# Key sums taken two groups after their loads, transposes alternating with A·V, and half of the last batch's groups turned by DMA alone

## The chip, the cores and the metric

The kernel runs on 1 core of one Trainium2 chip. The time is that of the whole launch on the device, in microseconds (us), and each kernel has the median of several runs. The profile shows one more execution, whose span goes from the first to the last instruction on the core. Engines are named as in the profile: PE (TensorE matmuls), PEld (TensorE weight loads), DVE (VectorE), ACT (ScalarE), POOL (GpSimd), and SP (SyncE, whose queue issues every DMA here).

## What is computed

Attention against keys that are pooled 4x4 and projected (768 keys for 12288 queries, width 128, 4 batches), followed by a gated block: a causal convolution of 5 taps with a sigmoid makes a gate for a projected value.

```python
# attention
kv_pool = kv.reshape(B, H // 4, 4, W // 4, 4, C).mean(axis=(2, 4))
k = v = kv_pool.reshape(B, -1, C) @ w_sr          # 768 rows
s = (q @ k.transpose(0, 2, 1)) / np.sqrt(C)
s = s - s.max(-1, keepdims=True)
a = np.exp(s)
a /= a.sum(-1, keepdims=True) + 1e-09
x = a @ v                                          # (4, 12288, 128)
# gated block
gate_pre = sum(conv_w[k] * xp[:, k:k + S] for k in range(5))   # xp: 4 zeros ahead of x
out = (1 / (1 + np.exp(-gate_pre))) * (x @ w_val) @ w_out
```

## The kernel before

**Groups and steps.** The queries of a batch are cut into 24 groups of 512, so there are 96 groups. One loop over `t` runs 4 steps (`j` = 0 to 3) for each group `gi`; a step handles 128 queries against all 768 keys. The program is written in the order in which each engine shall work (`manual_schedule`): every engine takes its instructions in the order of the code, and waits where an operand or a buffer isn't ready. Everything is pipelined over groups: while the scores of group `gi` are softmaxed (`cur`), group `gi`-2 goes through A·V (`avg`), `gi`-3 through the convolution (`xg`) and `gi`-4 through the gated block (`mg`).

**One step.** `score` makes the 128x768 scores of the *next* step in 6 matmuls (q and k are split into a high and a low part), into one of three pairs of PSUM banks (tile `s`, pool `ps_s`, `bufs=3`). So the scores of step 2 take the pair that step 3 of the group before had. `row_max` (DVE, tile `nm`) finds the maxima, `expo` (ACT) the exponentials. `p_hi` (ACT) and `p_lo` (DVE, one step later) split the probabilities into two fp16 parts; `p_lo` is the last reader of `s` and sets its bank pair free.

**Turning.** A·V needs the probabilities with the keys on partitions. Steps 0 to 2 are turned by DMA: `p_hi` and `p_lo` write tile `hl`, and a `dma_start_transpose` on SP's queue writes tile `pt` (steps 0 and 1 together, step 2 alone). Step 3 is turned on PE: `expo` writes `pf` in SBUF, and `turn` transposes its six 128x128 blocks back into the bank pair, from where `p_hi` and `p_lo` write `pt`. `on_pe(j)` is `j >= 3`.

**A·V.** 18 fp16 matmuls for a group add up in one bank (`av`). `AV_CUTS` spreads them over the four steps: 7, 2, 3 and 6. After the last, `g_x` (DVE) makes `x` from `av`.

**PE's order.** In step 0: scores, 7 of A·V, and one small transpose of the row sums (`norm_turn`, tiles `z` to `m`). Step 1: scores, the value projection `g_val` (tile `m`, L388), 2 of A·V. Step 2: scores, the output projection `g_out` (L398), 3 of A·V. Step 3: scores, 6 of A·V, the six turns (L298). `g_val`, `g_out` and `norm_turn` share one PSUM bank (pool `ps_m`, `bufs=1`); `norm_store` (DVE, tile `r`) must have read the row sums before `g_val` may write.

**DVE's order.** Step 0: `row_max`, reciprocal, `p_lo` of step 3, and, when a later batch is being prepared, `pool_kv`. Step 1: `row_max`, `r`, `p_lo`, `g_h` (tile `h`, which needs `g_val`). Step 2: `row_max`, `p_lo`. Step 3: `row_max`, `p_lo`, `g_x`. ACT's order in steps 2 and 3 is `expo`, `p_hi`, the cast of a later group's queries (`g_qh`), `expo`.

**Keys of the next batch.** `setup_steps` makes a list of steps, one of which is taken at the end of each group: 16 pieces, which load part of kv (`load_kv`, tile `kvt`) and return the sum over 16 neighbours (`pool_kv`, L121, tile `pool`) as work for step 0 of the next group; then the projections and the splitting of keys and values. The first piece loads three pieces, so its sum stands one step behind its own load. The first batch's keys are made ahead of the loop. `load_moe` returns 14 small DVE instructions that convert the block's weights from 64-bit words (`convert`); 8 of them stand among the sums of the first batch, and 6 are handed out from step 6 on (`trickle`, two in a step).

Of the kernel before, what the change touches and what calls it, by code (L numbers as in the profile page):

```python
# [8 lines left out]
F16 = mybir.dt.float16  # L9
# [7 lines left out]
P = 128  # L17
GQ = 512
NT = GQ // P
NX = 3  # L20


class Group:
# [4 lines left out]
def attn_moe_kernel(ctx, tc, qT, kvT, w_sr, w_moe, outT):  # L28


    nc = tc.nc
    B, C, N = qT.shape
    RR = R * R
    NK = kvT.shape[2] // RR
    NCH = NK // P
# [3 lines left out]
    TAPS = NW - 2 * C  # L39
    HALO = TAPS - 1  # L40
    PIECES = 16
    AV_CUTS = (0, 7, 9, 12, 18)
    assert 3 * NCH == AV_CUTS[-1]
    PC = NK // PIECES
    AHEAD = 5
# [6 lines left out]
    hlp = ctx.enter_context(tc.tile_pool(name="hlp", bufs=2))  # L52
# [10 lines left out]
    def misc():  # L63
        return ps_m.tile([P, GQ], F32, name="m")
# [51 lines left out]
    def load_kv(b, st, i):  # L116
        st["kv", i] = kvp.tile([C, PC * RR], F32, name="kvt", bufs=AHEAD)
        nc.sync.dma_start(out=st["kv", i], in_=kvT[b, :, i * PC * RR:(i + 1) * PC * RR])

    def pool_kv(st, i):  # L120
        nc.vector.tensor_reduce(out=st["pool"][:, i * PC:(i + 1) * PC],  # L121
                                in_=st.pop(("kv", i)).rearrange("c (k s) -> c k s", s=RR),
                                axis=AX.X, op=ALU.add)

    def key_tiles(st):
        st["pool"] = keys.tile([C, NK], F32, name="pool", bufs=1)
        for n in ("kh", "kl"):
            st[n] = keys.tile([C, NK], F32R, name=n)
        for n in ("vh", "vl"):
            st[n] = keys.tile([P, NK], F16, name=n)  # L130
        st["vt"] = keys.tile([C, NK], F32, name="vt", bufs=1)

    def project(st, h, m):
        nc.tensor.matmul(m[:, :HALF], wsr, st["pool"][:, h * HALF:(h + 1) * HALF],
                         start=True, stop=True)
        st["m"] = m[:, :HALF]
# [55 lines left out]
        return high, low  # L192

    trickle = []

    def value_steps(st):
        return [lambda: trickle.extend(column_scale(st)), lambda: None, lambda: None,
                lambda: values(st, 0, misc()) or split_values(st, 0),
                lambda: values(st, 1, misc()) or split_values(st, 1)]

    def setup_steps(b, st):
        def piece(i):
            if i == 0:
                key_tiles(st)
            for k in range(3) if i == 0 else (i + 2,):
                if k < PIECES:
                    load_kv(b, st, k)
            return None, lambda: pool_kv(st, i)

        steps = [lambda i=i: piece(i) for i in range(PIECES)]  # L210
        steps += [lambda h=h: project(st, h, misc()) or split_keys(st, h) for h in range(2)]
        return steps + value_steps(st)

# [27 lines left out]
    def halves(a):  # L241
        return a.rearrange("p (h k) -> p h k", h=2)
# [11 lines left out]
    def row_max(g, j):  # L254
        nm = small.tile([P, 1], F32, name="nm")
        nc.vector.tensor_reduce(out=nm, in_=g.s[j], axis=AX.XY, op=ALU.max, negate=True)  # L256
        g.nm[j] = nm

    def on_pe(j):

        return j >= NX

    def expo(g, j):
        if j == 0:
            g.z = zs[g.i % len(zs)]
        if on_pe(j):
            g.pf[j] = pfp.tile([P, NK], F32, name="pf")
        nc.scalar.activation(out=halves(g.pf[j]) if on_pe(j) else g.s[j], in_=g.s[j],  # L268
                             func=AF.Exp, bias=g.nm.pop(j), accum_out=g.z[:, j:j + 1])

    def norm_eps(g):
# [18 lines left out]
        row = g.rd.rearrange("(o j) p -> o (j p)", o=1)  # L290
        nc.sync.dma_start(out=g.rb, in_=row.broadcast_to([C, GQ]))

    def turn(g, j):

        pf = g.pf.pop(j)
        for k in range(NCH):
            c = k % (NCH // 2) * P
            nc.tensor.transpose(g.s[j][:, k // (NCH // 2), c:c + P], pf[:, k * P:(k + 1) * P],  # L298
                                ident)

    def pt_tile(g):
        if g.pt is None:
# [2 lines left out]

    def part(g, j, a):

        if on_pe(j):
            return pt_tile(g)[:, j, a * NCH:(a + 1) * NCH].rearrange("p (h k) q -> p h (k q)", h=2)
        if g.hl is None:  # L310
            g.hl = hlp.tile([P, NX, 2, NK], F16, name="hl")
        return halves(g.hl[:, j, a])

    def p_hi(g, j):
# [2 lines left out]
    def p_lo(g, j):  # L317

        nc.vector.scalar_tensor_tensor(out=part(g, j, 1), in0=g.s.pop(j), scalar=2.0 ** 15,  # L319
                                       in1=part(g, j, 0), op0=ALU.mult, op1=ALU.subtract)  # L320
        if j in (1, 2):
            j0 = 0 if j == 1 else j
            nc.sync.dma_start_transpose(
                out=pt_tile(g)[:, j0:j + 1].rearrange("p j k q -> p (j k) q"),
                in_=g.hl[:, j0:j + 1].rearrange("p j a k -> p (j a k)"))
# [3 lines left out]
    def av_range(g, out, lo, hi, j0=0, j1=NT):  # L329
        for i in range(lo, hi):  # L330
            v, k, a = AV_ORDER[i]
            nc.tensor.matmul(out, g.st[v][:, k * P:(k + 1) * P], g.pt[:, j0:j1, a * NCH + k],  # L332
                             start=(i == 0), stop=(i == len(AV_ORDER) - 1))

    def av_part(g, part):
        if part == 0:
            g.av = ps_av.tile([C, GQ], F32, name="av")
        av_range(g, g.av, AV_CUTS[part], AV_CUTS[part + 1])

    def new_x(g, prev, copy):  # L340
        g.x = xp.tile([C, HALO + GQ], F32, name="x")
# [55 lines left out]
    def g_out(h, m):  # L397
        nc.tensor.matmul(m, wout, h, start=True, stop=True)  # L398
        return m
# [20 lines left out]
    for b in range(B):  # L420
        for i in range(NG):
            g = Group()
            g.i, g.b, g.t0, g.st = len(groups), b, i * GQ, states[b]
            g.s, g.nm, g.pf, g.hl, g.pt = {}, {}, {}, None, None
            groups.append(g)
    G = len(groups)
# [5 lines left out]
    st = states[0]  # L432
# [8 lines left out]
    for i in range(PIECES):  # L441
        if i + AHEAD < PIECES:
            load_kv(0, st, i + AHEAD)
        if i == 3:
            convert = load_moe()
        pool_kv(st, i)
        if i >= 8 and convert:
            convert.pop(0)()
        if i == 3 * PIECES // 4:
            low()  # L450
        if i % (PIECES // 2) == PIECES // 2 - 1:
            h = 2 * i // PIECES
            project(st, h, bank_pair()[:, 0])
            high, low = split_keys(st, h)
            high()
# [7 lines left out]
    steps = value_steps(st)  # L463
# [6 lines left out]
    for t in range(NT * G):  # L470
        gi, j = divmod(t, NT)
        cur, prev, nxt = (at(u // NT) for u in (t, t - 1, t + 1))
        last, avg, xg, mg, og = (at(gi - d) for d in (1, 2, 3, 4, 5))
        if j == 2 and gi % 2 == 0 and at(gi + 4):
            load_pair(at(gi + 4), at(gi + 5))
        if gi % NG == 1 and j == 0 and at(gi + NG - 1):
            steps += setup_steps(cur.b + 1, states[cur.b + 1])
        if t == NT + 2:
            trickle += convert

        if nxt:
            score(nxt, (j + 1) % NT)
        if mg and j == 1:
            mg.m = g_val(mg, misc())
        if mg and j == 2:
            mg.m = g_out(mg.h, misc())
        if avg:
            av_part(avg, j)

        if high and (j == 0 or t < NT):  # L490
            high()
            high = None
        row_max(cur, j)
        expo(cur, j)
        if on_pe(j):
            turn(cur, j)
            norm_eps(cur)
            if mg:
                out_tile(mg)
                g_evac(mg, mg.m)  # L500
        p_hi(cur, j)
        if mg and j == 0:
            mg.th = g_tanh(mg.gate)
        if xg and j == 1:
            tap(xg, TAPS - 1, nc.scalar)
        if last and j == 0:
            norm_reciprocal(last)
        if last and j == 1:
            norm_store(last)
        drip()  # L510
        if prev:
            p_lo(prev, (j - 1) % NT)
        if low and (j == 0 or t < NT):
            low()
            low = None
        if last and j == 0:
            norm_turn(last, misc())
        drip()
        if mg and j == 1:
            mg.h = g_h(mg.th, mg.m)  # L520
        if avg and j == 3:
            new_x(avg, xg, nc.gpsimd.tensor_copy)
            g_x(avg, avg.av)
        if xg and j == 1:
            g_conv(xg)
        if last and j == 3:
            norm_rows(last)
        if at(gi + 2) and j == 2:
            g_qh(at(gi + 2))
            g_ql(at(gi + 2))  # L530
        if og and j == 0 and og.i % 2:
            store_pair(og)
        if steps and (j == 3 or t < NT):
            high, low = steps.pop(0)() or (None, None)
# [20 lines left out]
    for i in (1, 2, 3):  # L555
        av_part(n2, i)
# [61 lines left out]
```

## Time and profile before

| | |
|---|---|
| median of 3 runs | 1132.18 us (1131.02 to 1132.25) |
| the profiled execution: its time | 1133.22 us |
| its span | 1131.4 us |
| PE busy | 1063.6 us, 94% of the span |
| DVE, ACT, POOL busy | 919.0, 910.4, 864.4 us (81%, 80%, 76%) |
| mean granted TensorE clock | 0.983 |
| DMA: share of the 16 engines | 85.4%, mean 190 GB/s |

A busy PE is not PE at its peak: matmuls overlap in the records. What a piece of work costs on PE is read from the chain of waits, which strings PE's pieces together end to start. An engine's idle time ahead of an instruction stands behind it in brackets in the timeline, with the engine that ended it; where that engine had long been done, it was another.

### The profile page before, as it was taken

How to read it: one execution, taken by the hardware profiler on the slowest of the kernel's cores; microseconds unless marked ns; L12 is line 12 of the kernel's file. 1: busy time of each engine (PE TensorE's matmuls, PEld its weight loads, DVE VectorE, ACT ScalarE, POOL GpSimd, SP SyncE). 2: the span in 40 equal slices, each digit the busy share in tenths (PEclk: the TensorE clock that was granted, in tenths of full speed). 3: DMA queues.
4: the chain of work that ended last, by engine and by line, in shares of the span. 5: the costliest groups of instructions: out<-in, count | busy, mean ns of one | idle time of the engine just before them, and what ended most of it. 6: DMA issues, size and time to landing. Idle time of an engine off the chain costs nothing.

```text
span 1131.4 us, 16595 instructions
## 1 busy us (share of the span) xinstructions
PE 1063.6 (94%) x5174; PEld 715.6 (63%) x5174; DVE 919.0 (81%) x1290; ACT 910.4 (80%) x1659; POOL 864.4 (76%) x948
## 2 busy tenths in 40 slices
PE   2879999999979999999997999999999999999996
PEld 1656666666756666666764666666666666666663
DVE  6868888888858888888885888888888888888884
ACT  1868888888858888888885888888888888888881
POOL 1168788878858888888885888887888888888872
PEclk9989999999989999999998999999999999999998
DMA  7779999887879999888876999898788888888872
GB/s 271 145 178 200 211 210 232 192 178 191 187 169 198 202 224 214 206 177 191 187 165 170 209 217 226 200 221 183 171 171 197 187 170 202 186 170 199 175 148 93
DMA packets 487095, 215.53 MB, mean 190 GB/s; under 512 B 453088, under 2 KB 453856, under 8 KB 487008
## 3 DMA queue, kind: packets, MB, share of 16 engines
q1 hardware_dynamic: 487008, 214.48, 85.4%
q8 instruction: 41, 0.67, 0.2%
q14 instruction: 46, 0.38, 0.1%
HBM read 75.83 MB, written 25.36 MB: 89 GB/s over the span
## 4 chain that ended last, share of the span: by engine, by line
PE 49%; DVE 25%; ACT 11%; issue 6%; POOL 5%; DMA 3%; SPq 1%; DVEq 0%; ACTq 0%
PE s L250 17%; PE av L332 16%; PE m L388 8%; DVE nm L256 8%; POOL ql L236 5%; ACT s L268 5%; DVE pool L121 4%; DVE pt L319 4%; ACT hl L315 4%; DVE x L349 4%; PE m L398 3%; PE s L298 3%; DMA kvt<-in_kv 3%; ACT qh L232 2%; DVE h L393 2%
## 5 line engine op out<-in xcount | busy, mean ns | idle before, releaser
L368 POOL TENSOR_TENSOR sum<-sum,tap 128x512 f32<-128x512 f32 x282 | 359.6, 1275 | 39.7 <-ACT tap L357 17.8
L332 PE MATMUL av<-pt,vh 128*128 128x512 f16 x1140 | 389.1, 383 | 0.0
L256 DVE TENSOR_REDUCE nm<-s 128x1 f32<-128x768 f32 x384 | 364.4, 949 | 3.7 <-PE s L250 3.7
L268 ACT ACTIVATE s<-s,nm 128x768 f32<-128x768 f32 x288 | 251.9, 875 | 125.5 <-DVE nm L256 124.3
L359 POOL TENSOR_SCALAR tap<-x,wm 128x512 f32<-128x512 f32 x376 | 253.4, 693 | 82.4 <-DVE x L349 80.9
L319 DVE SCALAR_TENSOR_TENSOR hl<-s,hl 128x768 f16<-128x768 f32 x288 | 273.1, 948 | 21.0 <-ACT hl L315 20.3
L250 PE MATMUL s<-kh,qh 128*128 128x384 f32 x768 | 253.3, 411 | 10.8 <-DVE hl L319 8.1
L315 ACT ACTIVATE hl<-s 128x768 f16<-128x768 f32 x288 | 233.3, 810 | 9.1
L332 PEld LDWEIGHTS <-vh 128*128 128x128 f16 x1164 | 114.0, 98 | 175.5 <-issue 85.8
L332 PE MATMUL av<-pt,vl 128*128 128x512 f16 x570 | 217.5, 382 | 0.0
L236 POOL TENSOR_TENSOR ql<-q,qh 128x512 fp32r<-128x512 f32 x96 | 121.8, 1269 | 122.6 <-ACT qh L232 122.6
L250 PE MATMUL s<-kh,ql 128*128 128x384 f32 x768 | 199.1, 341 | 0.0
L250 PE MATMUL s<-kl,qh 128*128 128x384 f32 x768 | 198.9, 340 | 0.0
L250 PEld LDWEIGHTS s<-kh,qh 128*128 128x128 f32 x768 | 132.4, 193 | 51.8 <-DVE hl L319 8.4
L349 DVE SCALAR_TENSOR_TENSOR x<-av,down,rb 128x512 f32<-128x512 f32 x95 | 71.4, 751 | 89.6 <-POOL ql L236 71.5
L250 PEld LDWEIGHTS s<-kl,qh 128*128 128x128 f32 x768 | 141.3, 190 | 0.5 <-DVE kl L147 0.5
L250 PEld LDWEIGHTS s<-kh,ql 128*128 128x128 f32 x768 | 140.9, 190 | 0.0
L388 PE MATMUL m<-x,wm 128*128 128x512 f32 x188 | 103.0, 630 | 25.0 <-DVE r L285 24.9
L368 POOL TENSOR_TENSOR sum<-tap,tap 128x512 f32<-128x512 f32 x94 | 120.4, 1281 | 0.0
L393 DVE SCALAR_TENSOR_TENSOR h<-th,m 128x512 f32<-128x512 f32 x94 | 64.7, 689 | 59.2 <-PE m L388 57.7
L315 ACT ACTIVATE pt<-s 128x768 f16<-128x768 f32 x96 | 77.8, 810 | 37.8 <-PE s L298 37.8
L332 PEld LDWEIGHTS <-vl 128*128 128x128 f16 x582 | 57.6, 99 | 77.9 <-issue 55.2
(68 smaller groups left out, 1068.9 us busy)
## 6 DMA issues: line engine op xcount, KB each, us to landing
kvt<-in_kv SPq DMA_DIRECT2D x64, 384.0 KB
rb<-rd SPq DMA_DIRECT2D x96, 256.0 KB
q<-in_q SPq DMA_DIRECT2D x47, 512.0 KB
out<-o SPq DMA_DIRECT2D x46, 512.0 KB
pt<-hl SPq DMA_TRANSPOSE x192
rd<-r SPq DMA_DIRECT2D x96, 2.0 KB
out<-o SPq DMA_DIRECT2D x3, 256.0 KB
q<-in_q SPq DMA_DIRECT2D x2, 256.0 KB
```

The lines of the kernel that those rows point to most:

```text
L236: nc.gpsimd.tensor_tensor(out=g.ql, in0=g.q, in1=g.qh.bitcast(F32), op=ALU.subtract)
L250: nc.tensor.matmul(s[:, h, :HALF], a[:, sl], k[:, h * HALF:(h + 1) * HALF], start=(i == 0), stop=(i == 2))
L256: nc.vector.tensor_reduce(out=nm, in_=g.s[j], axis=AX.XY, op=ALU.max, negate=True)
L268: nc.scalar.activation(out=halves(g.pf[j]) if on_pe(j) else g.s[j], in_=g.s[j], func=AF.Exp, bias=g.nm.pop(j), accum_out=g.z[:, j:j + 1])
L315: nc.scalar.activation(out=part(g, j, 0), in_=g.s[j], func=AF.Copy, scale=2.0 ** 15)
L319: nc.vector.scalar_tensor_tensor(out=part(g, j, 1), in0=g.s.pop(j), scalar=2.0 ** 15, in1=part(g, j, 0), op0=ALU.mult, op1=ALU.subtract)
L332: nc.tensor.matmul(out, g.st[v][:, k * P:(k + 1) * P], g.pt[:, j0:j1, a * NCH + k], start=(i == 0), stop=(i == len(AV_ORDER) - 1))
L349: nc.vector.scalar_tensor_tensor(out=g.x[:, HALO + c0:HALO + c1], in0=av, scalar=g.st["down"], in1=g.rb[:, c0:c1], op0=ALU.mult, op1=ALU.mult)
L359: eng.tensor_scalar(out=g.tap[k], in0=src, scalar1=w, scalar2=1.0, op0=ALU.mult, op1=ALU.mult)
L368: nc.gpsimd.tensor_tensor(out=s, in0=acc, in1=g.tap[k], op=ALU.add)
L388: nc.tensor.matmul(m, wval, g.x[:, HALO + c0:HALO + c1], start=True, stop=True)
L393: nc.vector.scalar_tensor_tensor(out=h, in0=th, scalar=1.0, in1=m, op0=ALU.add, op1=ALU.mult)
```

## The change

It has five parts.

1. `pool_kv` no longer stands in step 0 right after its load. A piece's sum is put into a list when the next piece is loaded, and one sum is taken from the list in each step 2. A sum so comes two groups behind its load, and the list of steps is one longer (17 pieces).
2. `AV_CUTS` goes from 7, 2, 3, 6 to 6, 2, 2, 8 matmuls in steps 0 to 3.
3. The six turns of step 3 no longer follow the A·V matmuls: each of them is issued behind one of the last six.
4. In the last batch, every second group (0, 2, 4 ...) is turned by DMA in all four steps; its steps 2 and 3 go together. Tile `hl` holds four steps now.
5. The 14 converting instructions all stand in the loop, from step 4 on.

```diff
-    AV_CUTS = (0, 7, 9, 12, 18)
+    AV_CUTS = (0, 6, 8, 10, 18)
...
         def piece(i):
             if i == 0:
                 key_tiles(st)
+            else:
+                pooling.append(lambda: pool_kv(st, i - 1))
             for k in range(3) if i == 0 else (i + 2,):
                 if k < PIECES:
                     load_kv(b, st, k)
-            return None, lambda: pool_kv(st, i)
-        steps = [lambda i=i: piece(i) for i in range(PIECES)]
+        steps = [lambda i=i: piece(i) for i in range(PIECES + 1)]
...
-        return j >= NX
+        return j >= g.by_dma
...
-        if j in (1, 2):
-            j0 = 0 if j == 1 else j
+        if (j % 2 or j == g.by_dma - 1) and not on_pe(g, j):
+            j0 = j // 2 * 2
...
+        lo, hi = AV_CUTS[part], AV_CUTS[part + 1]
+        for i in range(lo, hi):
+            av_range(g, g.av, i, i + 1)
+            if hi - i <= len(between):
+                between.pop(0)()
...
+            g.by_dma = 4 if b == B - 1 and i % 2 == 0 else 3
...
-        if i >= 8 and convert:
-            convert.pop(0)()
...
-        if t == NT + 2:
+        if t == 3:
             trickle += convert
...
+        row_max(cur, j)
+        expo(cur, j)
+        turns = turn_steps(cur, j) if on_pe(cur, j) else []
         if avg:
-            av_part(avg, j)
+            av_part(avg, j, turns)
...
+        if pooling and j == 2:
+            pooling.pop(0)()
```

What this does to the engines' queues is seen at three places. First PE in step 3 of a group in the middle of the program. `av<-pt,vh` and `av<-pt,vl` are A·V matmuls with the high and low part of the values, each behind its weight load, `s<-ident,pf` a turn, `s<-kh,qh` the first matmul of the next scores. Before, the last three of step 3's six A·V matmuls, the turns, and the next scores:

```order
L332 LDWEIGHTS vh
L332 MATMUL av<-pt,vh 128x512
L332 LDWEIGHTS vl
L332 MATMUL av<-pt,vl 128x512
L332 LDWEIGHTS vh
L332 MATMUL av<-pt,vh 128x512
L298 MATMUL s<-ident,pf 128x128 [waits Activation_49]
L298 MATMUL s<-ident,pf 128x128 x5
L250 MATMUL s<-kh,qh 128x384 [waits DVE_49,PE_49]
```

After, the first four of step 3's eight, with the first turns between:

```order
L251 MATMUL s<-kh,ql 128x384
L336 LDWEIGHTS vl
L336 MATMUL av<-pt,vl 128x512
L336 LDWEIGHTS vh
L336 MATMUL av<-pt,vh 128x512
L336 LDWEIGHTS vh
L336 MATMUL av<-pt,vh 128x512
L300 MATMUL s<-ident,pf 128x128 [waits Activation_49]
L336 LDWEIGHTS vl
L336 MATMUL av<-pt,vl 128x512
L300 MATMUL s<-ident,pf 128x128
```

The first turn, which waits for ACT's exponentials, stood behind six A·V matmuls of its step and now stands behind three; five A·V matmuls stand behind it.

Second DVE, from `p_lo` of step 3 (`pt<-s,pt`) to the next `g_x` (`x`), while a later batch's keys are summed. `nm` are the row maxima, `hl<-s,hl` the other `p_lo`. Before:

```order
L319 SCALAR_TENSOR_TENSOR pt<-s,pt 128x768
L121 TENSOR_REDUCE pool<-kvt 128x48
L256 TENSOR_REDUCE nm<-s 128x1
L285 COPY r<-m 4x128
L319 SCALAR_TENSOR_TENSOR hl<-s,hl 128x768
L393 SCALAR_TENSOR_TENSOR h<-th,m 128x512
L256 TENSOR_REDUCE nm<-s 128x1
L319 SCALAR_TENSOR_TENSOR hl<-s,hl 128x768
L256 TENSOR_REDUCE nm<-s 128x1
L319 SCALAR_TENSOR_TENSOR hl<-s,hl 128x768
L349 SCALAR_TENSOR_TENSOR x<-av,down,rb 128x512
```

After:

```order
L323 SCALAR_TENSOR_TENSOR pt<-s,pt 128x768
L257 TENSOR_REDUCE nm<-s 128x1
L286 COPY r<-m 4x128
L323 SCALAR_TENSOR_TENSOR hl<-s,hl 128x768
L404 SCALAR_TENSOR_TENSOR h<-th,m 128x512
L257 TENSOR_REDUCE nm<-s 128x1
L323 SCALAR_TENSOR_TENSOR hl<-s,hl 128x768
L120 TENSOR_REDUCE pool<-kvt 128x48
L257 TENSOR_REDUCE nm<-s 128x1
L323 SCALAR_TENSOR_TENSOR hl<-s,hl 128x768
L360 SCALAR_TENSOR_TENSOR x<-av,down,rb 128x512
```

The sum of keys moved from ahead of `r` to ahead of the row maxima of step 3.

Third PE in step 3 of a group of the last batch that has no turns, after the change: the end of the eight A·V matmuls.

```order
L336 LDWEIGHTS vl
L336 MATMUL av<-pt,vl 128x512
L336 LDWEIGHTS vh
L336 MATMUL av<-pt,vh 128x512
L251 MATMUL s<-kh,qh 128x384 [waits DVE_49,PE_49]
```

Before the change this place read like the first listing above.

More of the change, by code (lines that the diff above doesn't have):

```diff
@@ L19 @@
 NT = GQ // P
-NX = 3
 class Group:
@@ L194, in attn_moe_kernel @@
     trickle = []
+    pooling = []
     def value_steps(st):
@@ L257, in row_max, with on_pe @@
         g.nm[j] = nm
-    def on_pe(j):
-        return j >= NX
+    def on_pe(g, j):
+        return j >= g.by_dma
     def expo(g, j):
@@ L265, in expo @@
             g.z = zs[g.i % len(zs)]
-        if on_pe(j):
+        if on_pe(g, j):
             g.pf[j] = pfp.tile([P, NK], F32, name="pf")
-        nc.scalar.activation(out=halves(g.pf[j]) if on_pe(j) else g.s[j], in_=g.s[j],
+        nc.scalar.activation(out=halves(g.pf[j]) if on_pe(g, j) else g.s[j], in_=g.s[j],
                              func=AF.Exp, bias=g.nm.pop(j), accum_out=g.z[:, j:j + 1])
@@ L291, in norm_rows, with turn_steps, block @@
         nc.sync.dma_start(out=g.rb, in_=row.broadcast_to([C, GQ]))
-    def turn(g, j):
+    def turn_steps(g, j):
         pf = g.pf.pop(j)
-        for k in range(NCH):
+        def block(k):
             c = k % (NCH // 2) * P
@@ L299, in turn @@
                                 ident)
+        return [lambda k=k: block(k) for k in range(NCH)]
     def pt_tile(g):
@@ L306, in part @@
     def part(g, j, a):
-        if on_pe(j):
+        if on_pe(g, j):
             return pt_tile(g)[:, j, a * NCH:(a + 1) * NCH].rearrange("p (h k) q -> p h (k q)", h=2)
         if g.hl is None:
-            g.hl = hlp.tile([P, NX, 2, NK], F16, name="hl")
+            g.hl = hlp.tile([P, NT, 2, NK], F16, name="hl")
         return halves(g.hl[:, j, a])
@@ L333, in av_range, with av_part @@
                              start=(i == 0), stop=(i == len(AV_ORDER) - 1))
-    def av_part(g, part):
+    def av_part(g, part, between=()):
         if part == 0:
             g.av = ps_av.tile([C, GQ], F32, name="av")
-        av_range(g, g.av, AV_CUTS[part], AV_CUTS[part + 1])
+        lo, hi = AV_CUTS[part], AV_CUTS[part + 1]
[3 more added lines that the diff above has]
+                between.pop(0)()
+        for matmul in between:
+            matmul()
     def new_x(g, prev, copy):
@@ L486, in attn_moe_kernel @@
             mg.m = g_out(mg.h, misc())
+        row_max(cur, j)
+        expo(cur, j)
+        turns = turn_steps(cur, j) if on_pe(cur, j) else []
         if avg:
-            av_part(avg, j)
+            av_part(avg, j, turns)
+        else:
+            for matmul in turns:
+                matmul()
         if high and (j == 0 or t < NT):
@@ L492, in attn_moe_kernel @@
             high = None
[L493 to L496, printed above, removed]
+        if j == NT - 1:
             norm_eps(cur)
```

## The prediction

> **What bounds the kernel now.** I read the page first (PE busy 94% of the span, the others 76 to 81%), then the chain of waits to see whether PE works without a break, and then the timeline of one group for the queues behind PE. From the chain of waits, one whole group of the last batch, from one set of turns to the next (start, length, piece):
>
> ```profile
> 1070.46 1.05 PE s L250 x6
> 1071.51 1.53 PE av L332 x7
> 1073.04 0.11 PE m L278
> 1073.14 1.07 PE s L250 x6
> 1074.21 0.86 PE m L388 x2
> 1075.07 0.43 PE av L332 x2
> 1075.51 1.05 PE s L250 x6
> 1076.55 0.86 PE m L398 x2
> 1077.41 0.65 PE av L332 x3
> 1078.06 1.05 PE s L250 x6
> 1079.11 1.31 PE av L332 x6
> 1080.42 0.66 PE s L298 x6
> 1081.08 1.05 PE s L250 x6
> ```
>
> PE's pieces follow each other with no hole: 10.62 us for a group (1070.46 to 1081.08). Scores are 1.05, an A·V matmul 0.218 (1.53 / 7), a turn 0.11 (0.66 / 6). PE is the bound here, but what matters for this change is how near the other engines run behind it. The timeline of another group of that batch, the rows that lead from the value projection to the turns:
>
> ```profile
> 904.04 1.02 PE L388 MATMUL m<-x,wm 128*128 128x512 f32 x2
> 905.17 0.69 DVE L393 SCALAR_TENSOR_TENSOR h<-th,m 128x512 f32<-128x512 f32 x1 [0.51 <-PE m L388]
> 905.77 0.95 DVE L256 TENSOR_REDUCE nm<-s 128x1 f32<-128x768 f32 x1
> 906.82 0.88 ACT L268 ACTIVATE s<-s,nm 128x768 f32<-128x768 f32 x1 [0.58 <-DVE nm L256]
> 907.50 0.95 DVE L256 TENSOR_REDUCE nm<-s 128x1 f32<-128x768 f32 x1
> 907.84 0.81 ACT L315 ACTIVATE hl<-s 128x768 f16<-128x768 f32 x1
> 908.55 0.61 ACT L232 CAST qh<-q 128x512 fp32r<-128x512 f32 x1
> 909.06 0.90 ACT L268 ACTIVATE pf<-s,nm 128x768 f32<-128x768 f32 x1
> 910.03 0.38 PE L332 MATMUL av<-pt,vh 128*128 128x512 f16 x1
> 910.10 0.72 PEld L298 LDWEIGHTS s<-ident,pf 128*128 128x128 f32 x6 [0.19 <-ACT pf L268]
> 910.24 0.82 PE L298 MATMUL s<-ident,pf 128*128 128x128 f32 x6
> 910.51 0.75 DVE L349 SCALAR_TENSOR_TENSOR x<-av,down,rb 128x512 f32<-128x512 f32 x1 [0.87 <-POOL ql L236]
> ```
>
> Read it as a chain: DVE waits 0.51 for the value projection before `h`; behind `h`, in DVE's order, come the maxima of step 2; ACT waits 0.58 for these, then does the exponentials of step 2, `p_hi`, the cast of q, and the exponentials of step 3 without a pause; the turns' weight load waits 0.19 for those. From the projection's start to the first turn it takes 910.24 - 904.04 = 6.20 us. PE's own work over the same stretch, from the chain of waits, is 0.86 + 0.43 + 1.05 + 0.86 + 0.65 + 1.05 + 1.31 = 6.21. So the data arrive just when PE has done its six A·V matmuls: there is no slack at all, though no wait of PE shows it.
>
> **Parts 2 and 3, the turns among A·V.** After the change PE reaches the first turn after 2 A·V matmuls in step 2 (one less) and 3 in step 3 (three less): 6.21 - 4 x 0.218 = 5.34 us. The exponentials still take 6.20, since nothing in their chain gets shorter. PE waits 0.86 at the first turn, and everything behind it in its queue (five A·V matmuls, then the scores) waits too. The wait isn't won back: the next projection stands behind the turns on PE, and the next exponentials behind the projection. It is a loop, 6.20 from projection to first turn, and then PE's path back: six turns 0.66, five A·V 1.09, scores 1.05, six A·V 1.31, the small transpose 0.11, scores 1.07 = 5.29. Together 11.49, against 10.62.
>
> In that path back stands a second wait. For it, the rows of DVE one group earlier:
>
> ```profile
> 899.90 0.75 DVE L349 SCALAR_TENSOR_TENSOR x<-av,down,rb 128x512 f32<-128x512 f32 x1 [0.87 <-POOL ql L236]
> 901.51 0.93 DVE L319 SCALAR_TENSOR_TENSOR pt<-s,pt 128x768 f16<-128x768 f32 x1
> ```
>
> `x` starts 0.48 after the last A·V matmul (910.03 to 910.51), and `p_lo` of step 3 starts 1.61 after `x` and takes 0.93. The last A·V matmul now starts 5 x 0.11 + 4 x 0.218 = 1.42 behind the first turn, so `p_lo` ends at 1.42 + 0.48 + 1.61 + 0.93 = 4.44 and its bank pair is free some 0.07 later, at 4.51. PE wants that pair for the scores of step 2 at 0.66 + 1.09 + 1.05 + 1.31 + 0.11 = 4.22: a wait of 0.29. A group with turns then takes 11.49 + 0.29 = 11.78, say 11.77 unrounded.
>
> Does alternating itself change PE's work? No row shows a turn between two A·V matmuls. The nearest is the small transpose behind seven A·V matmuls, 0.11 in the chain of waits, like a turn in a run; I take 0.11. From below, a turn streams 128 columns where an A·V matmul streams 512 in 0.218, so 0.054; from above I double it to 0.22 for the switching.
>
> The Trainium skill, "TensorE: Matmul & The Clock Gate", Step-by-step: what each phase is for, says that PE pulls weight loads ahead of matmuls in flight; by that a turn's weights would load behind A·V and the turn would cost its columns alone, which the first rival prices. The small transpose, which stands behind A·V and still takes 0.11, does not bear this out.
>
> **Part 1, the sums of keys.** Around the start of a batch's preparation the timeline shows:
>
> ```profile
> 317.56 0.75 DVE L349 SCALAR_TENSOR_TENSOR x<-av,down,rb 128x512 f32<-128x512 f32 x1 [0.87 <-POOL ql L236]
> 320.79 1.38 SPq L118 DMA_DIRECT2D kvt<-in_kv  x3
> 326.78 0.95 DVE L121 TENSOR_REDUCE pool<-kvt 128x48 f32<-128x768 f32 x1 [6.67 <-DMA kvt<-in_kv]
> 328.84 2.08 PE L388 MATMUL m<-x,wm 128*128 128x512 f32 x2 [6.97 <-DVE r L285]
> 337.66 0.75 DVE L349 SCALAR_TENSOR_TENSOR x<-av,down,rb 128x512 f32<-128x512 f32 x1 [2.11 <-issue]
> ```
>
> The list of waits has all of this kind (us in total, times, longest):
>
> ```profile
> DVE pool L121 <- DMA kvt<-in_kv: 25.2, 8, 7.0
> ```
>
> The sum waits 6.67 for a load issued 6 us before; DVE's whole queue waits behind it, then PE behind `r`, and PE starts again slowly (2.08 for a projection that takes 1.02 above). From `x` to `x` this group takes 20.10. Ordinary groups while keys are summed:
>
> ```profile
> 206.58 0.75 DVE L349 SCALAR_TENSOR_TENSOR x<-av,down,rb 128x512 f32<-128x512 f32 x1 [0.86 <-POOL ql L236]
> 209.04 0.94 DVE L121 TENSOR_REDUCE pool<-kvt 128x48 f32<-128x768 f32 x1
> 210.76 0.27 DVE L285 COPY r<-m 4x128 f32<-4x128 f32 x1
> 211.08 1.13 PE L388 MATMUL m<-x,wm 128*128 128x512 f32 x2 [0.20 <-DVE r L285]
> 217.68 0.75 DVE L349 SCALAR_TENSOR_TENSOR x<-av,down,rb 128x512 f32<-128x512 f32 x1 [0.89 <-POOL ql L236]
> ```
>
> take 11.10, since the sum delays `r` and PE waits for it. The stall is worth 20.10 - 11.10 = 9.0, three times (batches 2 to 4 are prepared in the loop): 27. Bounds: the bare waits, three of about 6.7 or 20, and 27; the first stall falls into the filling of the pipeline, where less is lost, so I take 26. Two groups are 22 us, over three times the 6 us that the load took, so no new wait takes its place on SP or DVE.
>
> The sum's new place costs something. In step 2 it stands ahead of the maxima of step 3, which started at 907.50. A sum takes DVE 0.86 to the next instruction; so they start at 908.36, end 0.95 later, and the exponentials, which started at 909.06, start at about 909.34: 0.28 more on the loop. A group with a sum takes 12.05. The wait for `r` goes: with the sum gone from ahead of it, `r` comes at the time that PE gets through the wait for the bank pair.
>
> **Part 4, the last batch.** A group without turns saves 0.66 and has no wait at a first turn. From the projection's start PE comes to the end of A·V at 0.86 + 0.43 + 1.05 + 0.86 + 0.44 + 1.05 + 8 x 0.218 = 6.43; `x` starts at 6.43 - 0.22 + 0.48 = 6.69, and `p_lo` of step 3 sets the bank pair free at 6.69 + 1.61 + 0.93 + 0.07 = 9.30. PE is there at 6.43 + 1.05 + 1.31 + 0.11 = 8.90, waits 0.40, and with 1.07 of scores the group takes 10.37. Alternating with 11.77, the mean is 11.07. The added transposes are a sixth more than now. In the table of windows the last batch's DMA share is the figure before the GB/s:
>
> ```profile
> 899.90:1070.00 170.10, 170.10 (x852) 116.78 (x850) 139.74 (x193) 149.33 (x273) 146.88 (x161) 1.00 0.86 184
> ```
>
> 0.86 while PE never stops; even if all of that were transposes, a sixth more would stand at 1.00 of the old group time, below 1.00 of the longer one. They are issued a whole group before A·V reads them, so I price them at 0.
>
> **Part 5, the conversions.** By group of lines:
>
> ```profile
> L90 DVE TENSOR_SCALAR rest<-raw 128x261 int32<-128x261 int32 x3 | 0.9, 287 | 0.0
> ```
>
> Eight such instructions leave the way to the first scores, 8 x 0.2 beyond what overlaps: at most 1.6 saved if DVE bounds there, 0 if the loads do; the same eight come back in the first groups. Between -1.6 and +1.6 I take 0.
>
> **The sum.** 48 groups with a sum (3 x 16): 12.05 - 11.10 = 0.95, +45.6. 24 groups of the last batch: 11.07 - 10.62 = 0.45, +10.8. About 20 others (92 groups have the loop, counted from the first with a value projection): before between 10.62 and 11.10, and as they too do extra work on DVE I take 11.10; 0.67 each, +13.4. Stalls at the three starts: -26. Together +44. The profiled execution took 1133.2 (span 1131.4), 1.0 above the median, so the median goes from 1132.2 to 1176.
>
> **The rivals.** *Hidden turns:* alternated turns cost 0.054. The last A·V matmul starts at 1.14, the bank pair comes at 4.23, and the loop is 6.20 + 4.23 + 1.07 = 11.50, 0.27 less in each of the 80 groups with turns (48 + 20 + 12): 1154. For it speaks only that streaming is no longer than that; against it the small transpose.
>
> *Costly switches:* five turns at 0.22 add 0.55 x 80 = 44: 1220. No row has a switching cost: A·V behind the output projection starts on time in the chain of waits.
>
> *No wait at the first turn* (faster): the exponentials are not tied to the projection, and move forward with PE. Then a group with turns is 10.62 + 0.29 = 10.91, with the wait for `r` gone: 48 x -0.19, 20 x -0.19, the last batch (10.91 + 10.37) / 2 = 10.64, +0.5, and -26 give -38: 1094. It is faster as long as the wait at the first turn is under 38 / 80 = 0.48 on the mean. For it: in the list of waits PE itself now hardly waits there. Against it: the unbroken rows from `h` to the turns.
>
> *The stalls stay:* if the sums still wait for their loads, +26: 1202. It would take loads of 20 us.
>
> **How the numbers follow.** Forecast 0.64, hidden turns 0.13, costly switches 0.09, no wait at the first turn 0.09, stalls that stay 0.02, about no change 0.03 (part of the wait, with free turns). 1176 is the first. The range reaches to hidden turns below and to half of the switching cost and the staying stalls above: 1150 to 1204. A change under 0.2% cannot be told from none here. Faster 0.10, same 0.02, slower 0.88.
>
> **What would show it.** The first turn's weight load should wait for ACT's `pf` about 1 us in 80 groups; `x` to `x` should be near 12.05 with sums, 11.8 without, and 10.4 and 11.8 by turns in the last batch; scores should wait 0.3 for `p_lo`; no sum should wait for its load in the loop. If PE shows no wait ahead of the turns, I am wrong on the loop; if the groups are right by number but 0.3 off, on the turns' cost.

## The result, and the profile after

The changed kernel takes 1202.29 us (median of 4 runs, 1201.38 to 1203.26) against 1132.22 for the kernel before: a ratio of 1.062, with a 95% interval from 1.0601 to 1.0638. The direction, the mechanism and the range (1150 to 1204) held; the point, 1176, was 26 us too low.

The head of its page:

```profile
span 1201.5 us, 16475 instructions
PE 1085.4 (90%) x5102; PEld 701.1 (58%) x5102; DVE 915.6 (76%) x1290; ACT 910.4 (76%) x1659; POOL 865.9 (72%) x948
```

Every engine has a smaller share of a longer span, which points to waits between them. Rows of the changed kernel's list of waits (us in total, times, longest):

```profile
PEld s L300 <- ACT pf L269: 95.4, 84, 1.6
PEld s L251 <- DVE pt L323: 30.8, 67, 0.6
PEld m L279 <- DVE kl L146: 9.1, 6, 1.5
PEld m L279 <- DVE vl L188: 7.9, 8, 1.3
DVE pool L120 <- DMA kvt<-in_kv: 5.6, 6, 2.8
```

The first row is the first turn (L300), which now waits for `pf` in every group with turns; its weight load did so for about 1.1 us each (95.4 / 84). The second row is the wait for the bank pair that `p_lo` of step 3 frees, 0.46 each. The next two rows were not in the prediction: the small transpose (L279) waits for the split of keys and values. The last was 25.2 before; what is left of it is the first batch, so the three stalls are gone.

The chain of waits in the last batch shows the loop whole, from one value projection (L399) to the next:

```profile
1097.39 0.87 PE m L399 x2
...
1098.35 0.69 DVE h L404
1099.04 0.88 DVE nm L257
...
1100.00 1.00 ACT s L269 x2
...
1101.03 0.81 ACT hl L319
1101.84 0.51 ACT qh L233
1102.35 0.90 ACT pf L269 x2
...
1103.29 0.33 PE s L300
1103.62 0.22 PE av L336
1103.84 0.11 PE s L300
...
1105.26 0.73 DVE x L360
...
1106.94 0.86 DVE pt L323
1107.84 1.31 PE s L251 x6
1109.15 0.86 PE m L399 x2
```

Down to `pf` it is the predicted chain: projection, `h`, maxima, exponentials, `p_hi`, the cast of q, exponentials. Then PE's turns alternate with A·V, and behind the last of them the chain leaves PE again: `x`, `p_lo` of step 3 (`pt`), and the scores that wait for its bank pair. From 1097.39 to 1109.15 is 11.76, where the prediction said 11.77.

How the 70 us (spans 1131.4 and 1201.5) come together, from the start of `x` in one group to its start in the next, in both traces:

| part of the program | predicted | measured |
|---|---|---|
| a group with a sum | 12.05 (was 11.10) | 12.05 |
| a group that only has turns | 11.77 (was 10.62) | 11.77 |
| last batch, with turns / all by DMA | 11.77 / 10.37 | 11.82 / 10.52 |
| groups with sums, the starts' included | +45.6 (48 groups) | about +48.6 (50 groups) |
| projecting keys and values, and their neighbours | +13.4 (20 groups at 0.67) | about +30 (21 groups at 1.44) |
| last batch | +10.8 | +13.1 |
| stalls at three starts | -26 | about -25 |
| up to the first `x` | 0 | +3.2 |

### The profile page after: what moved, and what is told of

Same layout as the page of the kernel before. It is cut to its first block, busy times and chain, and to the rows that moved or that the text cites. A ratio compares the mean times of both kernels' runs of the same rounds, so it can differ in the third digit from the quotient of the medians.

```text
span 1201.5 us, 16475 instructions
## 1 busy us (share of the span) xinstructions
PE 1085.4 (90%) x5102; PEld 701.1 (58%) x5102; DVE 915.6 (76%) x1290; ACT 910.4 (76%) x1659; POOL 865.9 (72%) x948
## 4 chain that ended last, share of the span: by engine, by line
POOL 32%; DVE 17%; PE 17%; issue 17%; ACT 15%; DMA 1%; POOLq 0%; DVEq 0%; ACTq 0%
POOL sum L379 15%; POOL tap L370 11%; DVE x L360 6%; PE s L251 5%; PE av L336 5%; POOL ql L237 5%; DVE nm L257 5%; ACT s L269 5%; ACT hl L319 4%; ACT pf L269 3%; PE s L300 3%; PE m L399 2%; DVE h L404 2%; DMA kvt<-in_kv 1%; ACT qh L233 1%
## 5 line engine op out<-in xcount | busy, mean ns | idle before, releaser
L336 PE MATMUL av<-pt,vh 128*128 128x512 f16 x1140 | 380.7, 381 | 0.1
L269 ACT ACTIVATE s<-s,nm 128x768 f32<-128x768 f32 x300 | 261.9, 873 | 114.1 <-DVE nm L257 101.3
L323 DVE SCALAR_TENSOR_TENSOR hl<-s,hl 128x768 f16<-128x768 f32 x300 | 284.4, 948 | 10.1 <-ACT hl L319 10.1
L251 PE MATMUL s<-kh,qh 128*128 128x384 f32 x768 | 246.0, 401 | 19.9 <-DVE hl L323 6.8
L319 ACT ACTIVATE hl<-s 128x768 f16<-128x768 f32 x300 | 243.4, 811 | 8.7
L300 PE MATMUL s<-ident,pf 128*128 128x128 f32 x504 | 141.2, 284 | 54.2 <-ACT pf L269 54.2
L251 PEld LDWEIGHTS s<-kh,qh 128*128 128x128 f32 x768 | 125.4, 191 | 102.1 <-DVE pt L323 30.8
L319 ACT ACTIVATE pt<-s 128x768 f16<-128x768 f32 x84 | 68.1, 811 | 111.5 <-PE s L300 111.5
L300 PEld LDWEIGHTS s<-ident,pf 128*128 128x128 f32 x504 | 71.0, 142 | 100.1 <-ACT pf L269 95.4
L336 PEld LDWEIGHTS <-vl 128*128 128x128 f16 x582 | 61.7, 106 | 67.6 <-issue 47.0
```

The costliest lines, as they stand in the source:

```text
L251: nc.tensor.matmul(s[:, h, :HALF], a[:, sl], k[:, h * HALF:(h + 1) * HALF], start=(i == 0), stop=(i == 2))
L269: nc.scalar.activation(out=halves(g.pf[j]) if on_pe(g, j) else g.s[j], in_=g.s[j], func=AF.Exp, bias=g.nm.pop(j), accum_out=g.z[:, j:j + 1])
L319: nc.scalar.activation(out=part(g, j, 0), in_=g.s[j], func=AF.Copy, scale=2.0 ** 15)
```

## The experiments

All were run beside the kernel before, which had medians from 1132.1 to 1133.6 in these comparisons. "A group" is `x` to `x`. The theory is the loop of the prediction; the main rivals are that turns cost something by themselves when they stand among A·V, that the sums' new place is what hurts, and that the wait at the first turn is the whole story.

**Which part does it.** First the sums alone: the kernel before with part 1.

```diff
+            else:
+                pooling.append(lambda: pool_kv(st, i - 1))
...
+        if pooling and j == 2:
+            pooling.pop(0)()
```

> The kernel before with part 1 alone: a sum of keys two groups behind its load, in step 2. Loop theory (the path from the value projection over h, the maxima, the exponentials to the first turn takes 6.20 us, and PE's way back sets the rest): the three stalls go (-26), and a group with a sum takes 6.20 + 0.28 + 4.42 = 10.90 instead of 11.10 (-0.2 x 48 = -10): 1096 us. Rival, the sum fits into idle time of DVE in step 2 and costs nothing: groups at 10.62, 1083 us. Rival, a sum in step 2 delays the turns by its full 0.86: 11.48, 1124 us.

Measured 1093.91, ratio 0.9664 (0.9649 to 0.9678). Part 1 alone is a gain of 38 us: the stalls go, and a group with a sum takes 10.83 in place of 11.10.

Then the changed kernel with its turns in a row behind the eight A·V matmuls, and the same with the old cuts, which leaves out parts 2 and 3 altogether (only the split `high` stays where the change put it):

```diff
-            if hi - i <= len(between):
-                between.pop(0)()
```

> The changed kernel with the six turns in a row behind all eight A.V matmuls of step 3 (cuts 6, 2, 2, 8 kept). Loop theory: PE reaches the first turn at 5.34 + 5 x 0.218 = 6.43 us after the projection, later than the 6.20 of the data, so the wait at the first turn goes, and x comes early enough that the bank pair isn't waited for: 10.62 without, about 10.68 with a sum, 10.5 on the mean in the last batch: about 1090 us. Rival, the cuts or the sums' place make the groups long: near 1200 us. Rival, alternating by itself costs PE time: both waits stay and only PE's own pieces get shorter, 1160 us.

```diff
-            if hi - i <= len(between):
-                between.pop(0)()
-    AV_CUTS = (0, 6, 8, 10, 18)
+    AV_CUTS = (0, 7, 9, 12, 18)
```

> The changed kernel without parts 2 and 3: cuts 7, 2, 3, 6 and the turns in a row. Loop theory: PE reaches the first turn at 6.21, the data are there at 6.20 without and 6.48 with a sum, so a group with a sum takes 10.90, 0.2 more than with cuts 6, 2, 2, 8 in a row: about 1097 us, 7 to 10 us slower than that kernel. Rival, the cuts make no difference when the turns stand in a row: the two are the same within 2 us.

Measured 1097.51 (ratio 0.9697, 0.9683 to 0.9712) and 1095.14 (0.9673, 0.9659 to 0.9687). Taking the alternation away gives back 105 of 1202 us, and with it the whole loss. But the second expectation had the order wrong: I thought the cuts 6, 2, 2, 8 would be 7 to 10 better, and they are 2.4 worse. They gain 0.15 in a group with a sum (10.68 against 10.83) and lose more elsewhere: 10.67 against 10.61 without one, 12.05 against 11.75 in a group that projects keys, 10.65 against 10.46 as the mean of twenty groups of the last batch. With one A·V matmul fewer in steps 0 and 2, PE comes to the next scores before `p_lo` has freed their banks; the list of waits of the run with 6, 2, 2, 8 in a row has it as

```profile
PEld s L251 <- DVE hl L323: 30.4, 91, 1.2
```

With the old cuts in a row this wait is 3.0 us in 5.

Parts 2 and 3 by themselves, on the kernel before (with the split `high` behind the exponentials, as the change's code has it):

> The kernel before with parts 2 and 3 alone (cuts 6, 2, 2, 8 and alternating turns); sums stay in step 0 right behind their loads, turns by DMA and conversions as before. Loop theory: p_lo of step 3 now ends 4.4 behind the first turn, the sum stands behind it and ahead of r, so the next projection can start 6.5 behind the first turn and the group with a sum takes 6.20 + 6.5 = 12.7; groups of the last batch 11.77. Against before: 45 x 1.6 = 72, 24 x 1.15 = 28, and 30 for the groups that project keys and values (three times the 10 that the changed kernel lost there): 1132 + 130 = 1262. Rival (the sums' new place is what lengthens their groups to 12.05, alternating alone leaves them at 11.77): 45 x 0.67 = 30 in place of 72, 1220.

Measured 1261.63, ratio 1.1141 (1.1122 to 1.116): 128 us slower. A group with a sum takes 12.63, one of the last batch 11.77. Where the sum stands decides what the alternation costs: in step 0 it holds `r`, and with it the projection from which the loop starts. Its weight load waits for `r` in the 15 ordinary groups with a sum from 70 to 300 us for 13.7 us in all, where it waited 7.7 in the kernel before; in the whole run, the starts included:

```profile
PEld m L397 <- DVE r L285: 54.5, 48, 6.3
```

Parts 4 and 5 by themselves, on the kernel before:

> The kernel before with part 4 alone (every second group of the last batch turned by DMA in all four steps). By the prediction's way of working, a group without turns saves 0.66 of PE and loses some to the wait for the bank pair. In the runs with turns in a row, two groups of the last batch take 10.60 + 10.28 against 2 x 10.61: 0.34 less for a pair, 12 pairs, 4.1 less: 1128. Rival (the added transposes get in the way of the others on the DMA queue, whose share in that batch was 0.86 already): no gain or a loss, 1132 or more.

> The kernel before with part 5 alone (all 14 conversions in the loop from step 4 on). The prediction took 0 between -1.6 and +1.6. The traces since show the first x 1.4 later where the conversions stand in the loop: 1133.6. Rival 1 (loads set the first scores, the groups that take the conversions have room): 1132. Rival 2 (the way to the first scores gets shorter by the eight conversions): 1130.6.

Part 4: 1127.92, ratio 0.9956 (0.9943 to 0.9968), a gain of 5.2; 3.6 of it lie in 21 groups of the last batch. Part 5: 1135.11, ratio 1.0021 (1.0011 to 1.003), a loss of 2.0; the first `x` comes 1.43 later. Rows of before, from its timeline and its windows (the granted clock stands ahead of the DMA share):

```profile
23.50 1.65 PE L134 MATMUL s<-pool,wsr 128*128 128x384 f32 x2 [7.98 <-DVE pool L121]
...
45.00:55.00 10.00, 9.28 (x53) 6.64 (x52) 9.90 (x17) 8.39 (x17) 1.26 (x1) 1.00 1.10 203
```

With part 5 alone:

```profile
22.14 1.65 PE L134 MATMUL s<-pool,wsr 128*128 128x384 f32 x2 [6.96 <-DVE pool L121]
53.78 0.88 ACT L268 ACTIVATE s<-s,nm 128x768 f32<-128x768 f32 x1 [1.39 <-DVE nm L256]
...
45.00:55.00 10.00, 9.21 (x43) 6.93 (x43) 8.62 (x17) 6.49 (x14) 0.73 (x1) 0.83 0.97 184
```

The projection of the first keys does start 1.36 earlier, as supposed. But the conversions now stand in DVE's queue while the pipeline fills: ACT waits 1.39 for maxima behind them, and PE has a granted clock of 0.83 in ten us where it had 1.00. By the first `x` more is lost than was gained; which of the two weighs more was not separated.

**What the loop is made of.** The theory says that it runs through ACT's cast of q, and that only in groups without a sum; with a sum the maxima of step 3 come last. So the cast (with `g_ql` on POOL, which reads it) is moved behind the exponentials of step 3, in the changed kernel:

```diff
-        if at(gi + 2) and j == 2:
-            g_qh(at(gi + 2))
-            g_ql(at(gi + 2))
...
         expo(cur, j)
+        if at(gi + 2) and j == 3:
+            g_qh(at(gi + 2))
+            g_ql(at(gi + 2))
         turns = turn_steps(cur, j) if on_pe(cur, j) else []
```

> The changed kernel, with the cast of the queries (g_qh on ACT and g_ql on POOL) moved from step 2 to step 3, behind the exponentials that the first turn waits for. Loop theory: without a sum the exponentials of step 3 then wait for the maxima alone, 0.5 less, so such groups take 11.27 in place of 11.77; with a sum the maxima of step 3 end at the same time as before, so those groups stay at 12.05. 12 alternating groups of the last batch and about 20 others x 0.5 = 16 less: 1186. Rival 1, the first turn isn't tied to ACT's order: no change, 1202. Rival 2, ACT's order alone sets the loop, with or without a sum: 80 x 0.5 less, 1162.

Measured 1186.00, ratio 1.0471 (1.045 to 1.0492): the loop's number. Groups with a sum stay at 12.05, those with turns only fall to 11.25. Its timeline:

```profile
1064.73 0.94 DVE L257 TENSOR_REDUCE nm<-s 128x1 f32<-128x768 f32 x1
1065.77 0.90 ACT L269 ACTIVATE pf<-s,nm 128x768 f32<-128x768 f32 x1
1066.65 0.62 ACT L233 CAST qh<-q 128x512 fp32r<-128x512 f32 x1
1066.81 0.33 PE L300 MATMUL s<-ident,pf 128*128 128x128 f32 x1
```

The exponentials follow the maxima at once, the cast comes after, and PE waits less at the first turn. Together with the 95.4 us of waits above, this rules out the rival in which the exponentials move with PE.

Then the other half of the claim, that a sum lengthens the loop since it stands ahead of those maxima. In the changed kernel the exponentials of such a group do wait for them:

```profile
212.02 0.90 ACT L269 ACTIVATE pf<-s,nm 128x768 f32<-128x768 f32 x1 [0.19 <-DVE nm L257]
```

The changed kernel with its sums in step 3, between `p_lo` and `x`:

```diff
-        if pooling and j == 2:
+        if pooling and j == 3:
```

> The changed kernel (alternating turns, cuts 6, 2, 2, 8) with the sum of keys in step 3, between p_lo and x, in place of step 2. Loop theory: the sum lay on the loop only since it stood ahead of the maxima of step 3 (0.28); DVE waits 2.17 for the last A·V ahead of x, so in the new place it is hidden and groups with a sum fall from 12.05 to 11.77: 48 x 0.28 = 13.4 less, 1189. Rival 1 (groups with a sum are long for POOL's taps or for another reason than the sum's place on DVE): 1202. Rival 2 (the sum holds x, and with it the bank pair of step 3): 1210.

Measured 1189.47, ratio 1.0495 (1.0474 to 1.0515). Groups with sums fall to 11.77, so it was the sum's place on DVE and not POOL's work that made them longer, and DVE still idles behind the sum:

```profile
209.67 0.94 DVE L120 TENSOR_REDUCE pool<-kvt 128x48 f32<-128x768 f32 x1
212.17 0.75 DVE L360 SCALAR_TENSOR_TENSOR x<-av,down,rb 128x512 f32<-128x512 f32 x1 [1.55 <-issue]
```

Is the wait at the first turn the whole story? If so, more A·V matmuls ahead of it should pay:

```diff
-    AV_CUTS = (0, 6, 8, 10, 18)
+    AV_CUTS = (0, 4, 5, 6, 18)
```

> The changed kernel with 4, 1, 1 and 12 A·V matmuls in steps 0 to 3 (in place of 6, 2, 2, 8); turns still alternate, now with the last six of twelve. Loop theory: PE reaches the first turn two A·V matmuls later, so its wait there falls from about 0.86 to 0.42; but the last turn and the last A·V come as before behind the first turn, and only 4 A·V matmuls are left in step 0 to hide p_lo, so the wait for the bank pair at the scores of step 2 grows from 0.29 to 0.73. The sum of the two waits stays, so group times stay at 11.77 and 12.05 and the time at 1202, within 6 us. Rival (only the wait at the first turn matters, the bank pair comes early enough): 80 groups x 0.44 less, 1167.

Measured 1217.96, ratio 1.0754 (1.0736 to 1.0771): slower than the change by 16, where I had said the same. The rival is refuted by far; the theory was right in part. Groups with a sum stay at 12.05 to the hundredth, since what PE no longer waits for at the turns it waits for at the scores:

```profile
PEld s L251 <- DVE hl L323: 116.5, 180, 1.2
PEld s L251 <- DVE pt L323: 43.2, 67, 0.7
PEld s L300 <- ACT pf L269: 22.1, 52, 1.2
```

Other groups took 0.16 more, and those turned by DMA alone 11.38 in place of 10.52, most of the 16 us. I had priced the bank pair of step 3 (`pt`) and not those of steps 0 to 2 (`hl`), which wait more than it does: with one A·V matmul each in steps 1 and 2, nothing covers `p_lo` there.

**The term that was too small.** In the changed kernel, a group that projects keys took 13.30:

```profile
276.53 0.75 DVE L360 SCALAR_TENSOR_TENSOR x<-av,down,rb 128x512 f32<-128x512 f32 x1 [2.41 <-PE s L300]
278.17 0.88 ACT L269 ACTIVATE s<-s,nm 128x768 f32<-128x768 f32 x1 [0.80 <-DVE nm L257]
279.06 0.48 ACT L142 ACTIVATE kh<-m 128x384 fp32r<-128x384 f32 x1
279.96 0.56 DVE L146 SCALAR_TENSOR_TENSOR kl<-m,kh 128x384 fp32r<-128x384 f32 x1 [0.89 <-ACT vt L143]
280.57 0.33 PE L279 MATMUL m<-ident,z 128*128 128x128 f32 x1 [1.03 <-DVE kl L146]
289.83 0.75 DVE L360 SCALAR_TENSOR_TENSOR x<-av,down,rb 128x512 f32<-128x512 f32 x1 [2.42 <-PE s L300]
```

The projected keys lie in the one small bank; `kh`, `vt` and `kl` read them, and the small transpose wants the same bank. In the changed code ACT does its exponentials first, which wait 0.80 for the maxima, and the split after them; before, the split went first. Put back:

```diff
+        if high and (j == 0 or t < NT):
+            high()
+            high = None
         row_max(cur, j)
         expo(cur, j)
...
-        if high and (j == 0 or t < NT):
-            high()
-            high = None
```

> The changed kernel with the block that splits projected keys and values (high, on ACT) put back ahead of the row maxima and the exponentials, as in the kernel before; the rest is as changed. Theory from the trace: the groups that project keys and values take 12.7 to 13.3 because that split now comes behind an exponential on ACT, so kl and vl are late and the small transpose, which shares their bank, waits. With the split ahead these groups should take 11.8 to 12.4: 12 groups x about 0.9 less, 1191 (1186 to 1195). Rival (what these groups lose comes from alternating itself): no change, 1202.

Measured 1191.55, ratio 1.052 (1.0501 to 1.0539). The group that took 13.30 takes 12.30, and PE hardly waits for `kl` (its weight load 3.3 us in the whole run, where it was 9.1):

```profile
275.71 0.75 DVE L360 SCALAR_TENSOR_TENSOR x<-av,down,rb 128x512 f32<-128x512 f32 x1 [2.41 <-PE s L300]
278.17 0.55 DVE L146 SCALAR_TENSOR_TENSOR kl<-m,kh 128x384 fp32r<-128x384 f32 x1
278.77 0.33 PE L279 MATMUL m<-ident,z 128*128 128x128 f32 x1
288.01 0.75 DVE L360 SCALAR_TENSOR_TENSOR x<-av,down,rb 128x512 f32<-128x512 f32 x1 [2.41 <-PE s L300]
```

**A better kernel.** The changed kernel without parts 2 and 3, and the sums in step 3:

```diff
-        if pooling and j == 2:
+        if pooling and j == 3:
```

> As the kernel with cuts 7, 2, 3, 6 and turns in a row, but the sum of keys stands in step 3, between p_lo and x, where DVE waits 0.87 for the end of A.V. Loop theory: the sum takes 0.86 there, the maxima of step 3 are no longer behind it, and a group with a sum takes 10.62 instead of 10.90: 48 x 0.28 = 13 us less, about 1084 us. Rival, DVE has no room left in any step (the sum only moves the wait to x): the same as with the sum in step 2, about 1097 us.

Measured 1083.89, ratio 0.9577 (0.9561 to 0.9593). Last, this with the split ahead of the maxima and the conversions among the first sums again:

> A version put together from the runs so far: the changed kernel with the turns in a row behind A·V and the cuts 7, 2, 3, 6 of before, the sum of keys in step 3 between p_lo and x, the conversions of the weights again among the first sums, and the split of projected keys and values (high) ahead of the maxima; the turns of the last batch by DMA as changed. Against the run with the sums in step 3 (1083.9): the first x should come 1.5 earlier, as it does where the conversions stand among the first sums; the groups that project keys should take 11.3 in place of 11.75, six groups x 0.45 = 2.7 less. 1079.7. Rival (neither place matters once PE doesn't wait at the turns): 1084.

Measured 1079.22, ratio 0.9526 (0.9512 to 0.9539): 54 us faster than the kernel before and 123 faster than the change. One of its groups with a sum:

```profile
202.64 0.94 DVE L120 TENSOR_REDUCE pool<-kvt 128x48 f32<-128x768 f32 x1
203.10 0.38 PE L336 MATMUL av<-pt,vh 128*128 128x512 f16 x1
203.32 0.82 PE L300 MATMUL s<-ident,pf 128*128 128x128 f32 x6
203.59 0.75 DVE L358 SCALAR_TENSOR_TENSOR x<-av,down,rb 128x512 f32<-128x512 f32 x1
214.20 0.75 DVE L358 SCALAR_TENSOR_TENSOR x<-av,down,rb 128x512 f32<-128x512 f32 x1
```

PE goes from A·V into the turns without a wait, the sum fills the time in which DVE waited for `x`, and the group takes 10.61: with a sum in it, what the kernel before took without one.

## Why the prediction was right, and where it was off

**The loop at the first turn: shown.** Both group times came out as predicted to the hundredth, the chain of waits goes through the named instructions, and the two runs that take one link out (the cast, the sum) moved just the groups that they should: 11.77 to 11.25 without a sum, 12.05 to 11.77 with one. What held was the step "there is no slack at all, though no wait of PE shows it". That the sums agree to the hundredth is in part luck: in the group of the chain above, the timeline has the first turn 6.06 behind the projection (1097.23 to 1103.29; the prediction said 6.20), the scores that wait for the bank pair 4.55 behind that (4.51), and the next projection 1.15 behind them (1.07). The prediction had read its 6.20 to the first turn, which stood behind PE's own A·V matmuls; the weight load, which waits for the data, started 6.06 behind the projection in the kernel before too (904.04 to 910.10). The differences cancel.

**What alternating costs by itself: nothing, nor does it save.** In the changed kernel's timeline:

```profile
213.23 0.38 PE L336 MATMUL av<-pt,vl 128*128 128x512 f16 x1
213.23 0.14 PEld L300 LDWEIGHTS s<-ident,pf 128*128 128x128 f32 x1
213.45 0.27 PE L300 MATMUL s<-ident,pf 128*128 128x128 f32 x1
213.56 0.38 PE L336 MATMUL av<-pt,vh 128*128 128x512 f16 x1
```

From a turn to the A·V matmul behind it is 0.11, as in a run. That disposes of both rivals on the turns' cost. The turn's weight load starts with the A·V matmul ahead of it (213.23), as the Trainium skill, "TensorE: Matmul & The Clock Gate", Step-by-step: what each phase is for, has it; yet the turn does not get cheaper.

**The stalls: right.** About 25 us came back (26 predicted). The rival in which they stay had 1202 for its time, which is what was measured; but no sum waits for its load inside the loop, so the number agrees by chance.

**The projecting groups: the term that was mis-sized.** About 20 groups at 0.67 each were to make +13.4; 21 groups made about 30. The prediction took 11.10 as their time before and 11.77 as that after. It had not asked where their extra work lies: before, those that project took 11.3, some 0.7 more than a group without, and in the loop the projection, issued behind the turns, stands on PE's path back, and most of the 0.7 comes on top of the 11.77 (12.30 with the split ahead). And the diff moved the split of keys and values on ACT, which the prediction did not price at all: 10.7 us (1202.29 - 1191.55), as the run with the split ahead shows. That 1202 still lies within the range is luck in part: its upper end was made of half a switching cost and of stalls that stay, and neither came.

**The first `x`: priced at 0, measured +3.2.** The bounds of -1.6 to +1.6 counted only the conversions' own time, once on each side. Part 5 alone makes 1.43 of it. In single executions of the changed kernel's other variants the first `x` stands at 58.04 without parts 2 and 3, at 58.99 with the cuts alone and at 59.48 with the alternation, against 56.30 before; the split put back leaves it at 59.66. So the cuts make about half of the rest; the alternation's share is no larger than what kernels with the same start differ by (59.48 to 60.09).

**The last batch: right but for 0.15** in the groups without turns (10.52, not 10.37), some 2 us in all. The added transposes, priced at 0, showed no cost of their own: part 4 alone gains, though the DMA share of that batch (880 to 1070 us) is then 1.00, where it was 0.86. In the changed kernel, whose groups are longer, it is 0.91 (the figure ahead of the GB/s):

```profile
899.00:1080.00 181.00, 172.81 (x812) 111.58 (x812) 140.51 (x195) 148.89 (x275) 146.50 (x160) 1.00 0.91 192
```

## What to carry to other kernels

On an engine that works in order, an instruction that waits for another engine should stand as late in its stretch as its consumers allow: moved ahead, it holds back all that stands behind it, and if that work feeds the one it waits for, the wait comes again in every turn of the loop and can't be won back. Before such a move, compare the two ways around (the busy engine's own work, and the chain through the others): equal lengths mean no slack, even where the list of waits shows none. And when a diff changes the order of the code, price every line that changes its place, also those that are no part of its description.

## What the hardware showed beyond that

A long wait costs PE more than its length. In the windows of the kernel before, the twenty us around a start have a granted clock (the figure ahead of the DMA share) of 0.83:

```profile
317.00:337.00 20.00, 13.03 (x55) 8.55 (x53) 9.65 (x13) 10.22 (x21) 9.74 (x12) 0.83 0.82 197
```

PE had waited 6.97 there, and the group lost 9.0.

Short waits left the clock alone where they were few, and not where they were dense. The changed kernel makes PE wait in nearly every group, for 1.6 us at the longest at the turns, and its last batch has 1.00 (the row above); over the whole run its mean clock is 0.994, against 0.983 before, though it is the slower one. But in the run with part 5 alone, while the pipeline fills, PE waited 0.94, 0.91 and 0.86 between 40 and 45.4 us and was busy for little more than half of that time. From 46 to 48 us the granted clock was then 0.50, and six turns took 1.54 in place of 0.82:

```profile
45.36 1.54 PE L298 MATMUL s<-ident,pf 128*128 128x128 f32 x6 [0.86 <-ACT pf L268]
```

From 36 us on, where the clock was 1.00, no wait of PE had been longer than 0.94. The Trainium skill, "TensorE: Matmul & The Clock Gate", What's actually happening, states that the clock falls to half after an idle window of some 3.4 us. The wait of 6.97 and the waits of the changed kernel's last batch agree with that; the fall behind waits of under 1 us does not follow from it, and there the measurement decides. No run here was made to find how much waiting it takes.
